# The order of the seven half products in a Strassen–Winograd second matmul: seventh product early, parts kept in the output blocks

## The chip, the cores and the metric

The kernel runs on one core of one Trainium2 chip. The metric is the device time of one execution in microseconds (us). An execution of it keeps five engines busy at once: PE (matmul), DVE (vector), ACT (activation), POOL (a second, slower vector engine) and SP, which here only issues DMAs. Each takes its own instructions strictly in the order in which the program lists them and waits on semaphores for the others.

## The reference

Eight batches of an attention between a block `x` (512 tokens, 8 heads of 64) and a state (32 rows) are computed in both directions, joined, and put through a two-layer MLP with SiLU:

```python
def _attn_ref(x, state):                       # x [8,8,512,64], state [8,8,32,64]
    scores = scale * np.matmul(x, state.transpose(0, 1, 3, 2))
    a = softmax(scores)
    xread = np.matmul(a, state)
    scores2 = scale * np.matmul(state, x.transpose(0, 1, 3, 2))
    a2 = softmax(scores2)
    sread = np.matmul(a2, x)
    return np.concatenate([xread, sread], axis=2)

def _moe_ref(x, w_in, w_out):                  # x [4352,512], w_in [512,2048], w_out [2048,512]
    h = x @ w_in
    g = h * (1.0 / (1.0 + np.exp(-h)))
    return g @ w_out
```

(The two softmaxes are written out in the original; they are shortened here.)

## The kernel before

**Units.** A batch's 512 rows of `xread` are one unit of work, b = 0 to 7; the rows of `sread` of all batches make a last, smaller unit 8. `w_in` is multiplied into the state beforehand: `W1[b]` = state times `w_in`, so the first matmul of the MLP is `aT[b]` (normalised attention weights, transposed) times `W1[b]`. It runs in 16 steps, "G1 steps" j = 0 to 15 (`upto`, `emit_G1`, L540): two matmuls of 512 columns into a PSUM tile `h1`, then one SiLU on ACT into `g` (L568). Tile `h1` has two buffers; a new step needs the buffer that is two steps old. The first eight SiLU results are the unit's `lo`, the other eight its `hi`.

**Second matmul.** For units 1 to 7 `g @ w_out` is done as seven half products (Winograd's form of Strassen's scheme), each 8 values of k with two matmuls of 256 columns (`Unit.mm`, L648): "a pair" below is these two matmuls. With A11, A21 the two halves of `lo` and A12, A22 those of `hi`, and S1 = A21 + A22, S2 = S1 − A11, S3 = A11 − A21, S4 = A12 − S2: P1 = A11·B11, P2 = A12·B21, P6 = S2·D2, P4 = A22·D4, P5 = S1·D1, P3 = S4·B22, P7 = S3·D3. The D's are differences of `w_out` (`t_weights`, tile `wt`), made once. S1 and S2 are tiles (`sums12`), S3 and S4 overwrite parts of `g` (`sums3`, `sums4`); all these sums run on DVE.

**PSUM.** P1, P6, P5 and P7 add up in one PSUM bank, `al`. P2, P4 and P3 each use the other bank, `be`, one after the other. After P1, P6 and P5 a copy of `al` is taken into an SBUF tile `snap` (`Unit.snap`); when a product in `be` is done, DVE adds it to a snap into a block of the unit's two output tiles `o_sb` (`block(i, c)`, 0 to 1 each). The last block, C22, is `al` after P7: `finish_last` copies it on ACT and adds on POOL, and this is done during the next unit's G1 steps (`j == lead + 1`). The banks have two tags, `o0` and `o1`; `al` takes the one with the unit's parity, so the roles swap from unit to unit.

**Order around a unit.** The program is scheduled by hand. In the G1 steps, `early` puts the pairs of P1 and then P2 between the steps. At the end come, in this order: the rest of P2; `group_a` (pieces of W1 for a later batch, `scores_t(m)`, and in some units `sread`) ahead of the last two pairs; P6; P4; P5; `group_b` (more pieces of W1); P3; P7. Six G1 steps of the next unit are put among the pairs of P3 and P7 (`LEADS = 6`). Unit 1 runs its `scores(2)` and `group_a` after P2 and P6, and units 1 and 7 have no `group_a` inside P2.

**Other work at fixed places of the G1 steps** (`j == lead + 1`, or right after unit 1's third step): on DVE `t_weights` (unit 1), `evict_state` (units 1 and 2), `norm_t(n)` (normalises the next unit's attention weights; one half runs on POOL), `spread_x`, `place_xm` (unit 7); on SP `fetch_x(m + 1)`, the load of a later `x`.

**SP's queue.** The loads of `x`, the stores of outputs (`out_half`) and all DMA transposes (`xT`, `aT`, `e`, `xs`) are issued by SP, one after the other; an entry whose semaphore has not come holds up all behind it. POOL casts the loaded `x` (`cast_x`, four instructions); SP then transposes it (`transpose_x`), and `scores_t` of that batch uses it.

Of the kernel before, what the change touches and what calls it, by code (L numbers as in the profile page):

```python
# [8 lines left out]
FP32 = mybir.dt.float32  # L9
# [9 lines left out]
B = 8  # L19
# [6 lines left out]
NFT = DF // 128  # L26
# [16 lines left out]
def kernel(  # L43
# [526 lines left out]
    def G2(b, tt, ft):  # L570
        if ft == 0:
            if b == 0 and tt >= 2:
                outs[tt] = psA.tile([128, DM], FP32, tag=f"a{tt - 2}", name="o_a")
            else:
                i = tt % 2
                outs[tt] = psO.tile([128, DM], FP32, tag=f"o{i}", name="o")
        nc.tensor.matmul(  # L577
            outs[tt][:],
            gt[b * NFT + ft][:, ds(128 * tt, 128)],
            w_out_sb[:, ft, :],  # L580
            start=(ft == 0),
            stop=(ft == NFT - 1),
            skip_group_check=True,
        )
# [23 lines left out]
    class Unit:  # L608
        def __init__(self, b):
            self.b = b  # L610
            self.lo, self.hi = gh[b, 0], None
            self.s1 = spool.tile([128, 8, 256], BF16, tag="s1", name="s1")
            self.s2 = spool.tile([128, 8, 256], BF16, tag="s2", name="s2")
            self.al = psO.tile([128, 2, 256], FP32, tag=f"o{b % 2}", name="o")
            self.be = None
            self.o = [
                opool.tile([128, 2, DM], FP32, tag=f"o_sb{i}", name="o_sb") for i in range(2)
            ]

        def snap(self, eng):  # L620
            t = spool.tile([128, 2, 256], FP32, tag=f"snap{len(self.kept) % 2}", name="snap")
            self.kept.append(t)
            copy(eng, t[:], self.al[:])

        kept = None

        def mm(self, p, k):
            hi, lo = self.hi, self.lo
            left, right = {
                1: (lambda: lo[:, k, 0:256], B11),  # L630
                2: (lambda: hi[:, k, 0:256], B21),
                3: (lambda: hi[:, k, 0:256], B22),
                4: (lambda: hi[:, k, 256:512], D4),
                5: (lambda: self.s1[:, k], D1),
                6: (lambda: self.s2[:, k], D2),
                7: (lambda: lo[:, k, 256:512], D3),
            }[p]
            left = left()
            if p in (2, 3, 4):
                if k == 0:  # L640
                    self.be = psO.tile(
                        [128, 2, 256], FP32, tag=f"o{1 - self.b % 2}", name="o"
                    )
                to, first = self.be, k == 0
            else:
                to, first = self.al, p == 1 and k == 0
            for t in range(2):
                nc.tensor.matmul(  # L648
                    to[:, t, :],
                    left[:, ds(128 * t, 128)],  # L650
                    right[:, k, :],
                    start=first and t == 0,
                    stop=(k == 7),
                    skip_group_check=True,
                )

        def sums12(self, k0, n):
            k = ds(k0, n)
            add(nc.vector, self.s1[:, k], self.lo[:, k, 256:512], self.hi[:, k, 256:512])
            sub(nc.vector, self.s2[:, k], self.s1[:, k], self.lo[:, k, 0:256])  # L660

        def sums4(self):
            for k0 in (0, 4):
                k = ds(k0, 4)
                sub(nc.vector, self.hi[:, k, 0:256], self.hi[:, k, 0:256], self.s2[:, k])

        def sums3(self):
            for k0 in (0, 4):
                k = ds(k0, 4)
                sub(nc.vector, self.lo[:, k, 256:512], self.lo[:, k, 0:256], self.lo[:, k, 256:512])  # L670

        def block(self, i, c):
            return self.o[i][:, :, ds(256 * c, 256)]
# [177 lines left out]

    PIECES_A = {1: 1, 2: 2, 3: 2, 4: 1, 5: 2, 6: 2}
    PIECES_B = {1: 3, 2: 3, 3: 3, 4: 3, 6: 2}
    LEADS = 6

    def finish_last(u):
        copy(nc.scalar, u.block(1, 1), u.al[:])
        add(nc.gpsimd, u.block(1, 0), u.block(1, 0), u.block(1, 1))
        u.out_half(1)

    def fetch_x(i):
        n = 4 if i < 6 else H
        for h in range(0, H, n):
            load_x(i, h, n, nc.sync)

    prev = None
    for b in range(1, B):
        n = b + 1
        m = n + 1
        u = Unit(b)  # L870
        u.kept = []
        lead = 3 if b == 1 else LEADS
        todo = [(1, k) for k in range(8)] + [(2, k) for k in range(8)]
        n_todo = len(todo)

        def early(j):
            while (
                todo
                and (8 * (todo[0][0] - 1) + todo[0][1]) <= j - 2
                and (n_todo - len(todo)) * (NFT - lead) < 13 * (j + 1 - lead)  # L880
            ):
                u.mm(*todo.pop(0))
                if len(todo) == 8:
                    u.snap(nc.vector)

        for j in range(lead, NFT):
            upto(NFT * b + j + 1)
            if j == 8:
                u.hi = gh[b, 1]
            if j == lead + 1:  # L890
                if prev is not None:
                    finish_last(prev)
                if b == 1:
                    transpose_x(3)
                    t_weights((2, 4, 3), 4, 4)
                    for v in range(2):
                        evict_state(v, nc.vector, 2, 2)
                    spread_x(2)
                elif n < B:
                    if b == 2:  # L900
                        for v in range(2):
                            evict_state(v, nc.vector, 4, 4)
                    norm_t(n)
                    spread_x(n)
                else:
                    for half in range(2):
                        place_xm(half, nc.vector)
                if 1 < b and m + 1 < B:
                    fetch_x(m + 1)
            early(j)  # L910
            if j == 13:
                u.sums12(0, 4)
        srs = SREAD_AT.get(b, ())

        def group_a():
# [3 lines left out]
            ps_sr = sread(srs, bank if m < B else new_h) if srs else None  # L919
            return pss, ps_sr  # L920

        u.sums12(4, 2)
        while todo:
            if len(todo) == 2 and 1 < b < B - 1:
                made = group_a()
            u.mm(*todo.pop(0))
        u.sums12(6, 2)
        add(nc.vector, u.block(0, 0), u.be[:], u.kept[0][:])
        if b == 1:
            for hg in range(2):  # L930
                scores(2, hg)
# [7 lines left out]
        if 1 < b and m + 1 < B:  # L939
            for c in range(4):  # L940
                cast_x(m + 1, nc.gpsimd, c, 1)
        def sread_g1(step):
            if n == B:
                upto(NFT * B + (step + 1) * NFT // 34)

        step = 0
        for k in range(8):
            u.mm(6, k)
            if n == B and k > 5:
                sread_g1(step)  # L950
                step += 1
        u.snap(nc.scalar)
        if b == 1:
            for hg in range(2):
                norm(2, hg)
# [1 line left out]
            made = group_a()  # L957
            exps_t(m)
            fetch_x(m + 1)
        if b > 1:  # L960
            u.sums4()
        if n < B:
            if m < B:
                nc.scalar.activation(warm[:], busy[:, 0:1], func=SILU, bias=0.0)
            w1_out(*made[0][0])
            if srs:
                sread_out(srs, made[1])
            for piece in made[0][1:]:
                w1_out(*piece)
        if b == 1:  # L970
            u.sums4()
        for k in range(8):
            u.mm(4, k)
            sread_g1(step)
            step += 1
        add(nc.vector, u.block(1, 0), u.be[:], u.kept[1][:])
        if 1 < b and m + 1 < B:
            transpose_x(m + 1)
        u.sums3()
        for k in range(8):  # L980
            u.mm(5, k)
            sread_g1(step)
            step += 1
        u.snap(nc.scalar)
        sub(nc.gpsimd, u.block(1, 0), u.block(1, 0), u.kept[2][:])
        if b in PIECES_B:
            c = PIECES_B[b]
            pss = w1_next(2) + (w1_next(1, new_h) if c == 3 else [])
            for i in (2, 0, 1)[3 - c :]:
                w1_out(*pss[i])  # L990
        for p in (3, 7):
            for k in range(8):
                u.mm(p, k)
                sread_g1(step)
                step += 1
                i = 8 * (p == 7) + k
                if n < B and i % 2 == 1 and 0 < i // 2 <= LEADS:
                    upto(NFT * n + i // 2)
            if b == 1 and p == 3:
                for c in range(4):  # L1000
                    cast_x(m + 1, nc.gpsimd, c, 1)
                transpose_x(m + 1)
            if p == 3:
                add(nc.vector, u.block(0, 1), u.be[:], u.kept[2][:])
                u.out_half(0)
        prev = u
        for ft in range(NFT):
            gt.pop(NFT * b + ft)
    finish_last(prev)
    for ft in range(NFT):  # L1010
        upto(NFT * B + ft + 2)
        G2(B, 0, ft)
# [32 lines left out]
```

## Time and profile before

| what | value |
|---|---|
| median of 3 runs | 203.37 us (203.17 to 203.37) |
| the profiled execution, its own time | 203.08 us |
| its span in the profile | 201.3 us |
| DVE busy | 126.9 us (63%) |
| ACT busy | 141.0 us (70%) |
| POOL busy | 60.8 us (30%) |
| G1 matmuls, L540, 252 of 512 columns | 73.8 us busy |
| half products, L648, 784 of 256 columns | 111.7 us busy |
| granted TensorE clock | 1.00 |

Busy times of matmuls overlap, since they are pipelined; the distance from the start of one to the start of the next tells their real price. Between two 512-column matmuls in a row it is 0.216 us, between two of 256 columns 0.109 us. So a G1 step costs PE 0.433 us, a pair 0.218 us, and a half product of eight pairs 1.75 us. The span leaves 1.8 us outside, which is the same work's start and end around the core's instructions.

### The profile page before, as it was taken

The numbers are of one execution on the slowest core, as the hardware profiler recorded it, in microseconds if no ns is written. First come the engines' busy times: TensorE is split into PE (matmuls) and PEld (weight loads), VectorE is DVE, ScalarE is ACT, GpSimd is POOL, SyncE is SP. The second block draws the span as 40 slices with busy tenths as digits, with TensorE's granted clock in tenths as the row PEclk, the third lists the DMA queues.
The fourth block names the chain that finished last, engine by engine and source line by source line (L and its number), as shares of the span: only waits on it lengthen the run. The fifth ranks groups of instructions, "written<-read, shape, count | busy, mean of one in ns | idle before, by whom it ended". The sixth has DMA issues, their size and how long they took to land.

```text
span 201.3 us, 4661 instructions
## 1 busy us (share of the span) xinstructions
PE 195.3 (97%) x1912; PEld 129.6 (64%) x1912; DVE 126.9 (63%) x244; ACT 141.0 (70%) x251; POOL 60.8 (30%) x79
## 2 busy tenths in 40 slices
PE   7799999999999999999999999999999999999992
PEld 2444445456866586668666776668666766688862
DVE  3862756999988797558864798187617972832101
ACT  2875667899787897789868777897784478545420
POOL 8674343730425504240804071400140022002020
PEclk9999999999999999999999999999999999999999
DMA  5999999994282797759164947142214020200222
GB/s 185 193 202 206 242 266 346 247 239 96 35 220 80 234 261 138 208 160 242 45 182 135 253 50 215 45 118 55 104 44 116 7 87 27 104 3 0 104 111 101
DMA packets 40965, 28.71 MB, mean 143 GB/s; under 512 B 27376, under 2 KB 37616, under 8 KB 40944
## 3 DMA queue, kind: packets, MB, share of 16 engines
q1 hardware_dynamic: 34736, 20.65, 38.4%
q0 software_dynamic: 5920, 7.64, 18.4%
q8 instruction: 15, 0.25, 0.5%
q10 hardware_dynamic: 288, 0.13, 0.3%
q14 instruction: 6, 0.05, 0.1%
HBM read 17.43 MB, written 8.91 MB: 131 GB/s over the span
## 4 chain that ended last, share of the span: by engine, by line
PE 94%; DMA 2%; DVE 1%; ACT 1%; issue 0%
PE o L648 43%; PE h L540 27%; PE o L577 5%; PE ps_w L473 5%; PE h L558 3%; PE o_a L577 3%; DMA x_f<-in_x_dram 2%; PE o_part L698 2%; PE ps_xt L257 1%; PE ps_sr L420 1%; PE ps_sc L310 1%; ACT xT L160 1%; PE ps_busy L168 1%; PE ps_scT L336 1%; PE ps_at L402 1%; PE h L522 0%
## 5 line engine op out<-in xcount | busy, mean ns | idle before, releaser
L568 ACT ACTIVATE g<-h 128x512 bf16<-128x512 f32 (+1 forms) x142 | 80.1, 575 | 29.0 <-PE h L540 20.1
L648 PEld LDWEIGHTS <-g 128*128 128x128 bf16 x560 | 53.7, 98 | 33.2 <-issue 3.1
L540 PE MATMUL h<-aT,W 128*128 128x512 bf16 x252 | 73.8, 379 | 0.1
L648 PE MATMUL o<-w_out_sb,g 128*128 128x256 bf16 x336 | 53.5, 273 | 0.1
L648 PE MATMUL o<-wt,g 128*128 128x256 bf16 x224 | 30.8, 273 | 0.0
L540 PEld LDWEIGHTS <-W 128*128 128x128 bf16 x252 | 24.4, 98 | 7.6 <-issue 0.7
L162 POOL CAST x_nat<-x_f 128x512 bf16<-128x512 f32 x24 | 17.4, 764 | 34.0 <-DMA x_f<-in_x_dram 28.3
L648 PE MATMUL o<-wt,s 128*128 128x256 bf16 x224 | 27.4, 273 | 0.0
L594 DVE TENSOR_TENSOR o_sb<-o,snap 128x512 f32<-128x512 f32 x21 | 14.5, 689 | 18.7 <-PE o L648 15.5
L162 DVE CAST W<-ps_w 128x512 bf16<-128x512 f32 (+1 forms) x35 | 21.8, 665 | 6.4 <-PE ps_w L473 6.4
L648 PEld LDWEIGHTS <-s 128*128 128x128 bf16 x224 | 21.9, 98 | 2.5
L591 POOL TENSOR_TENSOR o_sb<-o_sb,snap 128x512 f32<-128x512 f32 x7 | 8.9, 1269 | 37.3 <-ACT snap L160 37.3
L594 POOL TENSOR_TENSOR o_sb<-o_sb 128x512 f32<-128x512 f32 x7 | 8.9, 1266 | 36.7 <-ACT o_sb L160 36.7
L162 DVE COPY snap<-o 128x512 f32<-128x512 f32 x7 | 4.8, 691 | 23.3 <-PE o L648 19.1
L160 ACT ACTIVATE W<-ps_w 128x512 bf16<-128x512 f32 (+1 forms) x31 | 16.2, 580 | 2.8 <-PE ps_w L473 2.8
L160 ACT ACTIVATE snap<-o 128x512 f32<-128x512 f32 x14 | 8.4, 597 | 14.0 <-PE o L648 9.7
L577 PE MATMUL o<-w_out_sb,g 128*128 128x512 bf16 x48 | 13.2, 380 | 0.0
L577 PEld LDWEIGHTS <-g 128*128 128x128 bf16 x80 | 7.3, 98 | 8.7 <-issue 0.8
L594 DVE TENSOR_TENSOR s<-g 128x512 bf16<-128x512 bf16 (+1 forms) x21 | 11.5, 549 | 1.7 <-ACT g L568 1.6
L591 DVE TENSOR_TENSOR s<-s,g 128x512 bf16<-128x512 bf16 (+1 forms) x21 | 10.8, 514 | 0.7
L473 PE MATMUL ps_w<-w_in_sb,stT 64*32 64x512 bf16 (+1 forms) x264 | 10.2, 375 | 0.0
L591 DVE TENSOR_TENSOR g<-g 128x1024 bf16<-128x1024 bf16 x14 | 10.1, 759 | 0.0
(93 smaller groups left out, 191.6 us busy)
## 6 DMA issues: line engine op xcount, KB each, us to landing
out_dram<-o_sb SPq DMA_DIRECT2D x14, 512.0 KB, 2.8
x_f<-in_x_dram SPq DMA_DIRECT2D x6, 512.0 KB, 5.3
x_f<-in_x_dram POOLq DMA_DIRECT2D x2, 1024.0 KB, 11.6
x_f<-in_x_dram SPq DMA_DIRECT2D x2, 1024.0 KB, 6.5
w_out_sb<-in_moe_w_out_dram POOLq DMA_DIRECT2D x6, 256.0 KB, 11.3
w_in_sb<-in_moe_w_in_dram POOLq DMA_DIRECT2D x3, 512.0 KB, 10.6
out_dram<-o_sb SPq DMA_DIRECT2D x5, 256.0 KB, 5.7
x_f<-in_x_dram POOLq DMA_DIRECT2D x2, 512.0 KB, 14.6
```

The costliest lines, as they stand in the source:

```text
L160: nc.scalar.activation(dst, src, func=COPY, bias=0.0)
L162: eng.tensor_copy(dst, src)
L168: nc.tensor.matmul(ps[:], busy[:, 0:128], busy[:], start=True, stop=True, skip_group_check=True)
L473: nc.tensor.matmul(pss[f, hg][ds(32 * s, 32), 0:n], stT[ds(r, 64), b, h // 2, s % 2, :], w_in_sb[ds(r, 64), h // 2, ds(f, n)], start=True, ...
L540: nc.tensor.matmul(h_ps[k][:], W1[b][:, hg, ds(128 * ft, 128)], aT[b][:, hg, :, :], start=(hg == 0), stop=(hg == 1), skip_group_check=True,)
L558: nc.tensor.matmul(ps[:, 0:256], w_in_sb[:, kt, ds(128 * ft, 128)], xmT[:, :, kt].rearrange("p t n b -> p t (n b)"), start=(kt == 0), stop ...
L568: nc.scalar.activation(gt[k], ps[:, 0:n], func=SILU, bias=0.0)
L577: nc.tensor.matmul(outs[tt][:], gt[b * NFT + ft][:, ds(128 * tt, 128)], w_out_sb[:, ft, :], start=(ft == 0), stop=(ft == NFT - 1), skip_gr ...
L591: eng.tensor_tensor(dst, a, c, op=SUB)
L594: eng.tensor_tensor(dst, a, c, op=ADD)
L648: nc.tensor.matmul(to[:, t, :], left[:, ds(128 * t, 128)], right[:, k, :], start=first and t == 0, stop=(k == 7), skip_group_check=True,)
L698: nc.tensor.matmul(ps[:, 0:n], gt[b * NFT + ft][:, ds(128 * tt, 128)], w_out_sb[:, ft, cols], start=(ft == 0), stop=(ft == NFT - 1), skip_ ...
```

## The change

- P7 moves from the last place to the second: after P1, between the G1 steps, since it needs `lo` alone. It gets the bank `be`, which P2, P4 and P3 then use after it. `al` is always `o1` and `be` always `o0`.
- The difference for P7 (`sums3`) moves to the G1 steps: its first half at step 5, its second at step 9, on DVE. S2 is made directly from A22 − S3 in one instruction (`sums2`); S1 = S2 + A11 follows later (`sums1`, after P6's instructions).
- The snaps are gone: P1, P7, P6 and P5 are copied into the output blocks (`keep`), and later adds work in place. POOL adds P7 to U2 = P1 + P6 (`block(1, 0)`) and the copy of `al` after P5 to the P7 block. Stores go out in the same unit: half 1 after P5, half 0 after P3.
- Order at a unit's end: rest of P7; DVE copies P7; S2; `group_a` whole (units 2 to 6) with its evictions; all of P2; P6; P4; `group_b` (units 2 to 6; in unit 1 after P5); P5; P3. Five G1 steps of the next unit go in: one after P5, four among P3's pairs (unit 1: two after the second pair of P3).
- `fetch_x(m + 1)` moves from step 7 to step 5, ahead of `norm_t`'s transpose in SP's queue. The other work of step 7 moves to step 9; in unit 2 half of `evict_state` goes to POOL. In unit 1, D3 is made at step 5 and D2 and D4 at step 9, behind `evict_state` and `spread_x`.
- Unit 8's G1 steps in unit 7 are spread over 26 pairs instead of 34.

```diff
@@ Unit
-            self.al = psO.tile([128, 2, 256], FP32, tag=f"o{b % 2}", name="o")
+            self.al = psO.tile([128, 2, 256], FP32, tag="o1", name="o")
-        def snap(self, eng):
-            t = spool.tile([128, 2, 256], FP32, tag=f"snap{len(self.kept) % 2}", name="snap")
-            self.kept.append(t)
-            copy(eng, t[:], self.al[:])
+        def keep(self, eng, i, c):
+            copy(eng, self.block(i, c), self.al[:])
-            if p in (2, 3, 4):
+            if p in (7, 2, 4, 3):
                 if k == 0:
+                    self.be = psO.tile([128, 2, 256], FP32, tag="o0", name="o")
-        def sums12(self, k0, n):
-            add(nc.vector, self.s1[:, k], self.lo[:, k, 256:512], self.hi[:, k, 256:512])
-            sub(nc.vector, self.s2[:, k], self.s1[:, k], self.lo[:, k, 0:256])
+        def sums3(self, k0, n):
+            sub(nc.vector, self.lo[:, k, 256:512], self.lo[:, k, 0:256], self.lo[:, k, 256:512])
+        def sums2(self, k0, n):
+            sub(nc.vector, self.s2[:, k], self.hi[:, k, 256:512], self.lo[:, k, 256:512])
+        def sums1(self):
+            for k0 in (0, 4):
+                add(nc.vector, self.s1[:, k], self.s2[:, k], self.lo[:, k, 0:256])
@@ the G1 steps
-    LEADS = 6
+    LEADS = 5
-        todo = [(1, k) for k in range(8)] + [(2, k) for k in range(8)]
+        todo = [(p, k) for p in (1, 7) for k in range(8)]
-                and (n_todo - len(todo)) * (NFT - lead) < 13 * (j + 1 - lead)
+                and (n_todo - len(todo)) * (NFT - lead) < 16 * (j + 1 - lead)
                 u.mm(*todo.pop(0))
                 if len(todo) == 8:
-                    u.snap(nc.vector)
+                    u.keep(nc.vector, 0, 0)
-            if j == lead + 1:
-                if prev is not None:
-                    finish_last(prev)
+            if j == max(lead, 5):
                 if b == 1:
+                    t_weights((3,), 4, 4)
                     transpose_x(3)
-                    t_weights((2, 4, 3), 4, 4)
+                u.sums3(0, 4)
+                if 1 < b and m + 1 < B:
+                    fetch_x(m + 1)
+            if j == 9:
+                u.sums3(4, 4)
+                if b == 1:
                     for v in range(2):
                         evict_state(v, nc.vector, 2, 2)
                     spread_x(2)
+                    t_weights((2, 4), 4, 4)
                 elif n < B:
                     if b == 2:
                         for v in range(2):
-                            evict_state(v, nc.vector, 4, 4)
+                            evict_state(v, (nc.vector, nc.gpsimd)[v], 4, 4)
                     norm_t(n)
                     spread_x(n)
-                if 1 < b and m + 1 < B:
-                    fetch_x(m + 1)
             early(j)
             if j == 13:
-                u.sums12(0, 4)
+                u.sums2(0, 4)
@@ the end of the unit
-        u.sums12(4, 2)
         while todo:
-            if len(todo) == 2 and 1 < b < B - 1:
-                made = group_a()
             u.mm(*todo.pop(0))
-        u.sums12(6, 2)
-        add(nc.vector, u.block(0, 0), u.be[:], u.kept[0][:])
+        copy(nc.vector, u.block(1, 1), u.be[:])
+        u.sums2(4, 2)
+        if 1 < b < B - 1:
+            made = group_a()
+        u.sums2(6, 2)
+        if 1 < b < B - 1:
+            out_a()
+        for k in range(8):
+            u.mm(2, k)
+        add(nc.vector, u.block(0, 0), u.block(0, 0), u.be[:])
...
+        units(6)
+        u.keep(nc.scalar, 1, 0)
+        add(nc.gpsimd, u.block(1, 0), u.block(1, 0), u.block(1, 1))
         if b == 1:
             for hg in range(2):
                 norm(2, hg)
                 transpose_a(2, hg)
             made = group_a()
             exps_t(m)
             fetch_x(m + 1)
+            out_a()
+        u.sums1()
+        units(4)
+        add(nc.vector, u.block(1, 0), u.block(1, 0), u.be[:])
         if 1 < b and m + 1 < B:
             transpose_x(m + 1)
+        u.sums4()
+        if b > 1:
+            group_b()
+        units(5, {7: 1} if b > 1 else {})
+        u.keep(nc.scalar, 0, 1)
+        add(nc.gpsimd, u.block(1, 1), u.block(1, 1), u.block(0, 1))
+        u.out_half(1)
+        if b == 1:
+            group_b()
+        units(3, {1: 2, 3: 3, 5: 4, 7: 5})
+        if b == 1:
+            for c in range(4):
+                cast_x(m + 1, nc.gpsimd, c, 1)
+            transpose_x(m + 1)
+        add(nc.vector, u.block(0, 1), u.block(0, 1), u.be[:])
+        u.out_half(0)
```

`group_b` is now a small function with the same body; `out_a` holds the evictions of `group_a`; `units(p, leads)` issues the eight pairs of product p and, after the pairs named in `leads`, G1 steps of the next unit up to that number. The number of matmuls on PE does not change (3826 PE instructions, weight loads among them, in both).

## The prediction

> **What bounds the kernel now.** I read the page's busy times and chain first, then the order of time on each engine around the ends of units 1, 2 and 7.
>
> ```profile
> PE 195.3 (97%) x1912; PEld 129.6 (64%) x1912; DVE 126.9 (63%) x244; ACT 141.0 (70%) x251; POOL 60.8 (30%) x79
> PE 94%; DMA 2%; DVE 1%; ACT 1%; issue 0%
> ```
>
> PE sets the time: 94% of the chain that ended last. The change keeps every matmul, so it wins only what PE waits for today, and loses what it will wait for. PE's order of time at the end of unit 2:
>
> ```profile
> 68.19 0.38 PE L648 MATMUL o<-w_out_sb,g 128*128 128x256 bf16 x2
> 68.41 0.59 PE L540 MATMUL h<-aT,W 128*128 128x512 bf16 x2
> 68.84 0.60 PE L648 MATMUL o<-w_out_sb,g 128*128 128x256 bf16 x4
> 69.37 0.63 PE L473 MATMUL ps_w<-w_in_sb,stT 64*32 64x512 bf16 x16
> 69.81 0.40 PE L336 MATMUL ps_scT<-xT,stT 64*32 64x512 bf16 x8
> 70.15 0.61 PE L648 MATMUL o<-w_out_sb,g 128*128 128x256 bf16 x4
> ```
>
> Starts follow each other without a hole: G1 step 0.433, pair 0.218, `group_a` 0.87 (69.28 to 70.15, the entry of 0.09 included). Distances of starts beyond the usual 0.109 give what PE loses: 0.20 in unit 1 (at 47.06), 0.20 in unit 7 (174.35), where P2's last pair waits for the last SiLU with no `group_a` to cover it, and 0.09 in each of units 2 to 7 (64.75 the first), just behind `finish_last`'s ACT copy: 0.94 in all. **That is the whole prize** if every new wait is hidden.
>
> **The change, part by part.** Latencies from the trace: last matmul's start to a DVE instruction that waits for it 0.38 (58.24 to 58.62), to an ACT one 0.30 (49.71 to 50.01); engine to PE 0.05; G1 step's start to its SiLU's end 1.23 (173.38 to 174.61).
>
> (a) Removed: the 0.94. P2's end needs no fresh SiLU, and `finish_last` is gone from the G1 steps.
>
> (b) P7's copy now stands ahead of P2, in bank `o0`. PE could start P2 right after P7 in unit 7. From step 15: P7's last pair at 0.433, its second matmul at 0.54; DVE at 0.92; the copy 0.69 (as `snap` today), so P2 at 1.66, where PE was free at 0.65: 1.0 lost. With `group_a` (0.87) between, PE is free at 1.52: units 3 and 5 lose 0.14 each. Unit 4 has one piece of W1 only: its second `scores_t` tile waits for the last SiLU (1.28 after step 15 instead of 0.96), 0.3 lost. Unit 6 has `sread` as cover, none. Sum 1.6; bounds 1.2 (0.2 less in units 3 and 5 and in latencies) and 1.8.
>
> (c) Unit 1: the copy of P7 is behind a full DVE queue. Today:
>
> ```profile
> 39.62 1.93 DVE L591 TENSOR_TENSOR wt<-w_out_sb,wt 128x1024 bf16<-128x1024 bf16 x2
> 41.46 1.09 DVE L591 TENSOR_TENSOR wt<-w_out_sb 128x1024 bf16<-128x1024 bf16 x1
> 42.48 1.81 DVE L162 COPY stT<-st_x 64x64 bf16<-64x64 bf16 x8
> 44.32 0.69 DVE L162 COPY x_rows<-x_nat 128x2048 bf16<-128x2048 bf16 x1
> 44.93 0.68 DVE L162 COPY snap<-o 128x512 f32<-128x512 f32 x1
> 45.53 0.68 DVE L594 TENSOR_TENSOR s<-g 128x1024 bf16<-128x1024 bf16 x1
> ```
>
> DVE has no hole here. By these starts: D3 1.02, state copies 1.84, `x_rows` 0.61, D2 with D4 1.84, P1's copy 0.60, a half sum 0.71; half of `sums3` 0.64 (two take 1.28 in a row at 75.06). New order: D3 39.62 to 40.64, `sums3` first half to 41.3, then a hole: its second half needs SiLU 7, whose step starts at 41.11 (40.89 today, one pair more before it), so 42.4 to 43.05; state copies 44.9, `x_rows` 45.5, D2 and D4 47.35, P1's copy 47.95, `sums2` 48.65, P7's copy 49.35. PE finishes P7 at 47.40: step 15 is at 46.09 with 12 pairs before it and will have 15 (46.75), plus 0.433 and 0.218. P2 waits from 47.4 to 49.4: **2.0**. If D2 and D4 take 1.5 (the weights' group has a mean of 0.816, and POOL is silent then) 1.65. I take 2.0, the row itself.
>
> (d) `aT` for unit 2. Count from S, the end of P2 in unit 1, where `scores(2)` starts (S = 47.60 today). Today, POOL and then SP:
>
> ```profile
> 50.40 2.05 POOL L386 TENSOR_TENSOR an<-exp_nat,rc 128x512 bf16<-128x512 bf16 x2 [8.39 <-DVE rc L384]
> 62.70 3.20 POOL L162 CAST x_nat<-x_f 128x512 bf16<-128x512 f32 x4 [5.67 <-DMA xs<-xm]
> ```
>
> SP's own instructions in the same stretch (start, duration, what it issues):
>
> ```profile
> 51.48 3.73 SPq L396 DMA_TRANSPOSE aT<-an  x2
> 55.30 1.26 SPq L352 DMA_TRANSPOSE e<-eT  x1
> 56.65 1.11 SPq L112 DMA_DIRECT2D x_f<-in_x_dram  x2
> 57.86 3.67 SPq L448 DMA_TRANSPOSE xs<-xm  x3
> 65.93 1.65 SPq L147 DMA_TRANSPOSE xT<-x_nat  x1
> 67.68 1.01 SPq L676 DMA_DIRECT2D out_dram<-o_sb  x2
> ```
>
> The new POOL add of `block(1, 0)` stands ahead of both `an` in POOL's queue and waits for ACT's copy after P6: P6's last matmul S+2.11, copy S+2.41 to 3.01, add to 4.35 (1.27 as the POOL add at 55.73), first `an` to 5.4 (it ends at S+3.8 today), second to 6.4. SP: first transpose issued S+5.4 to 7.85 (2.42 today), second to 9.15, landed S+10.3 (2.35 after its issue, as today). PE reaches step 0 at S+9.05: `scores` 0.47, P6 1.75, `group_a` 1.53 (49.82 to 51.35), P4 1.75, P5 1.75, `group_b` 0.87, two pairs 0.44, and 0.48 before P5, since `sums1` is queued behind `sread_out`'s DVE work (S+5.25) and gives its first half at S+5.95. Step 0's second matmul, due S+9.26, waits till S+10.35. Together 0.48 + 1.08 = **1.55**. If the first transpose issues in 1.22 as the second does, all lands at S+9.1 and 0.48 is left. I take the same row's 2.42.
>
> (e) Unit 2: the longest new chain. P1's copy now writes the output tile, so it waits until unit 1's half 0 has been stored; behind it on DVE wait `sums2` and P7's copy, and P2 behind that. In SP's order the store stands behind the transpose `xT` of batch 4, which waits for POOL's cast, which waits for the load. Load: S+10.6 and 11.2 (SP after `aT` and `e`), landed 5.25 after the second issue (57.24 to 62.49 today): S+16.45. Cast from 16.65: 2.28 at best (four of 0.61, at 78.48), 3.20 above; I take 2.75, since DVE's `sums3` and `norm_t` run beside it as at 62.70. Transpose S+19.45 to 21.1, store issued 21.2, landed 3.2 later (67.68 to 70.79; 82.48 to 85.74) at 24.4. Then P1's copy 0.60, `sums2` 0.71, P7's copy 0.69, latencies 0.1: P2 at S+26.5. PE would be ready: step 0 ends S+10.55, step 1 10.98, three times (two pairs and a step) 0.87 gives step 5 at S+13.6; eleven steps and sixteen pairs 8.26; `group_a` 0.87: S+22.7. **3.75 lost**; bounds 3.15 (short issue, cast 2.28) and 4.2 (cast 3.20). The same wait hides that `xT` and half of `evict_state`, on POOL now (no row for such a copy there; DVE's are 0.27 each, POOL's casts of four times the length 0.61 to 1.07: 1 to 4 us for four), come late for `scores_t`: they would be done by S+23.8 at worst, and after the cover is gone would cost up to 0.6.
>
> The Trainium skill, "SBUF — State Buffer", section "Who interferes with whom", says that DVE and POOL share a port pair as an exclusive lock: DVE with two SBUF inputs blocks a POOL instruction that reads SBUF. The rows side with it only in part: a cast beside DVE's two-input work takes 1.07 instead of 0.61, not 0.61 plus the whole 0.76 of such a sum. By the rule the cast beside the moved `sums3` would take 0.3 more and the time with it; by the rows the 2.75 stands.
>
> (f) Later in unit 2: `cast_x(5)` is ahead of POOL's add. Its load is issued S+21.7 and 22.5, landed 28.4, cast to 30.9, add to 32.2, DVE's add in place 32.9, S4's halves 33.55 and 34.2, first W1 eviction 34.85. PE needs S4 for P3 after P5 and step 0 at S+34.8, and the evicted bank for step 1 at 35.2: nothing lost, 0.7 at the slow bounds. In units 3 and 4 the load goes out at step 6 and lands two us before the cast is due; S4 is ready 1.2 us ahead of P3, W1's bank 0.5 ahead of step 1. ACT in those units gives its copy after P6 in time for POOL. Nothing is charged there; the cover is P4, `group_b` and P5 (4.4 us).
>
> (g) In unit 7 the tail after P3 (16 matmuls of 0.216 and the `o_part` columns, 7 us) covers the last add and store; nothing.
>
> Sum: −0.94 + 1.6 + 2.0 + 1.55 + 3.75 = +8.0. The profiled execution took 203.08 (span 201.3, 1.8 around it), 0.3 under the median 203.37: 211.0 by the first, 211.3 by the second; I say **211.0**. Low ends: −0.94 + 1.2 + 1.65 + 0.48 + 3.15 = +5.5, 208.6; high: −0.94 + 1.8 + 2.0 + 1.55 + 4.2 + 0.7 = +9.3, 212.7.
>
> **Rivals.** First: the store of unit 1's half 0 is not late, so (e) falls to the plain 0.14 of (b). It takes a load landed and cast 3.6 us sooner. For it: DMA issues vary by two (1.22 and 2.42 for equal transposes), and the first `x` load before it took 4.1. Against: four waits in a row, each in program order. Then +4.4 or, with short issues, +3.0: 206.4 to 207.5. Chance 0.17.
>
> Second, faster: DVE is never the late one. The place is P2's start in units 1 to 7; the price is the 0.94 that (a) frees. It decides if P7's copy ends before PE is through `group_a` everywhere, that is, if the wait from P7 to P2 is 0.13 or less on average over seven units. For it: DVE is only 63% busy. Against: in unit 7 nothing stands between, and 0.38 + 0.69 cannot vanish; in unit 1 DVE has no hole. 202.4, chance 0.10, and 0.03 that gain and loss cancel.
>
> Third: (f) turns into a wait, the slow cast holding POOL's add, DVE's adds and S4 in unit 2 and again in 3, at 1 us or more each: above 213.1, chance 0.09.
>
> **Numbers.** Forecast 0.61 for 208.6 to 213.1, its own range. For 8 in 10 the range goes down over part of the first rival: 206.0 to 213.3. Faster by over 0.2% (the spread that runs of this kernel can tell from nothing) 0.10, within it 0.03, slower 0.87.
>
> **What would show it.** In the profile after: PE's largest waits before L642 at the start of P2 in unit 1 (2 us), unit 2 (3 to 4 us) and unit 7 (1 us), each ended by DVE's `o_sb<-o` copy; step 0 of unit 2 waiting for `aT`; DVE idle ahead of unit 2's first `o_sb` copy with a DMA as its releaser. Units 3 to 6 about as long as now. I am wrong if unit 2's copy of P1 finds its store landed, or if P2 in unit 1 starts before 48.

## The result, and the profile after

The changed kernel takes 211.16 us (median of 4 runs, 210.53 to 212.70) against 203.37 us before (203.17 to 203.81): a ratio of 1.039, 95% interval 1.033 to 1.045. The profiled execution took 212.70 us with a span of 210.8 us, 9.5 us more than the span before. Times of the experiments below are medians of all executions; their ratios leave out the slowest execution of e1, e5, e7 and e10, each over 1.5% longer than the fastest of its kernel, with a mean clock of 0.984 to 0.992.

The page's busy times, chain, and two rows of its 40 slices (5.3 us each; digits are tenths):

```profile
PE 197.8 (94%) x1893; PEld 131.3 (62%) x1912; DVE 133.3 (63%) x240; ACT 137.9 (65%) x244; POOL 64.1 (30%) x83
PE   7899999997899949999999999999999999899993
PEclk9999999999999966999999999999999999999999
PE 77%; DMA 11%; DVE 6%; POOL 2%; issue 1%; ACT 1%; POOLq 0%; DVEq 0%
```

PE's share of the chain fell from 94% to 77%; DMA, DVE and POOL stand in it now. PE is 40% busy in one slice, the 15th (73.8 to 79.0 us), and the granted clock is down in that slice and the next. Who PE waited for between 40 and 190 us (waiting instruction, releaser, us in total, times, longest):

```profile
PE o L642 <- DVE o_sb L162: 4.8, 3, 2.9
PE o L642 <- DVE s L594: 0.7, 2, 0.4
PE h L540 <- ACT W L160: 0.2, 1, 0.2
```

The three waits for DVE's copy of P7 are those of units 1, 2 and 7, as forecast. Unit 2 on PE, in order of time (start, duration, line, operation, count; in brackets the idle time before and what ended it):

```profile
72.38 0.38 PE L642 MATMUL o<-wt,g 128*128 128x256 bf16 x2
72.69 0.63 PE L473 MATMUL ps_w<-w_in_sb,stT 64*32 64x512 bf16 x16
73.13 0.50 PE L336 MATMUL ps_scT<-xT,stT 64*32 64x512 bf16 x8
76.52 3.57 PE L642 MATMUL o<-w_out_sb,g 128*128 128x256 bf16 x16 [2.89 <-DVE o_sb L162]
79.89 2.34 PE L642 MATMUL o<-wt,s 128*128 128x256 bf16 x10
```

DVE at the same time, in the same columns:

```profile
71.64 0.69 DVE L366 TENSOR_TENSOR an<-e,rcn 128x512 bf16<-128x512 bf16 x1
72.25 1.54 DVE L162 COPY x_rows<-x_nat 128x2048 bf16<-128x2048 bf16 x1
74.58 0.69 DVE L162 COPY o_sb<-o 128x512 f32<-128x512 f32 x1 [0.79 <-DMA out_dram<-o_sb]
75.19 0.68 DVE L591 TENSOR_TENSOR s<-g 128x1024 bf16<-128x1024 bf16 x1
75.79 0.69 DVE L162 COPY o_sb<-o 128x512 f32<-128x512 f32 x1
```

SP's DMA queue a little earlier (start, time that the issue holds the queue, line, operation):

```profile
68.95 1.69 SPq L147 DMA_TRANSPOSE xT<-x_nat  x1
70.74 0.54 SPq L673 DMA_DIRECT2D out_dram<-o_sb  x1
```

P1's copy (74.58) waits for the store that SP issued at 70.74 and that landed at 74.49; S2's first half and P7's copy (75.79) follow, and P2 starts at 76.52. Its 16 matmuls take 3.57 us instead of 1.91: each costs 0.213, twice the 0.109 of the page before. A table by stage (stretch, its length, then busy us of PE, weight loads, DVE, ACT and POOL, granted clock, DMA share, GB/s) shows why:

```profile
66.00:73.40 7.40, 7.35 (x68) 4.45 (x66) 6.11 (x9) 6.03 (x11) 5.89 (x9) 1.00 0.71 215
73.40:76.50 3.10, 0.23 (x8) 0.10 (x1) 2.31 (x5) 3.07 (x6) 0.00 (x0) 0.86 0.91 231
76.50:82.40 5.90, 5.88 (x28) 4.21 (x28) 4.00 (x7) 0.27 (x1) 2.28 (x4) 0.50 0.74 147
82.40:88.00 5.60, 5.55 (x66) 4.17 (x65) 2.88 (x5) 3.76 (x7) 1.27 (x1) 1.00 0.42 96
```

After the 3 us without a matmul, the clock is at 0.50 until 82.4: 27 matmuls (15 of P2, 12 of P6) lose 0.104 each, 2.8 us. The prediction's sum has no term for that.

The two other places. Unit 1, DVE ahead of P2:

```profile
45.72 1.41 DVE L591 TENSOR_TENSOR wt<-w_out_sb,wt 128x1024 bf16<-128x1024 bf16 x2
47.05 0.68 DVE L162 COPY o_sb<-o 128x512 f32<-128x512 f32 x1
47.65 0.68 DVE L591 TENSOR_TENSOR s<-g 128x1024 bf16<-128x1024 bf16 x1
48.25 0.68 DVE L162 COPY o_sb<-o 128x512 f32<-128x512 f32 x1
```

And PE in unit 1, with its waits in brackets:

```profile
47.51 0.38 PE L642 MATMUL o<-wt,g 128*128 128x256 bf16 x2
48.98 1.91 PE L642 MATMUL o<-w_out_sb,g 128*128 128x256 bf16 x16 [1.09 <-DVE o_sb L162]
56.70 1.05 PE L642 MATMUL o<-wt,s 128*128 128x256 bf16 x8 [0.30 <-DVE s L594]
58.16 1.05 PE L642 MATMUL o<-wt,s 128*128 128x256 bf16 x8 [0.41 <-DVE s L594]
```

Here P7's copy is the last of DVE's full queue, and P5 (56.70, 58.16) waits for both halves of S1. By distances of starts, the losses of PE are: P2 of unit 1 1.25, P5's halves 0.47 and 0.57, the first steps of unit 2 together 0.54, P2 of unit 2 2.96 and the half clock 2.8, unit 4's `scores_t` 0.31, P2 of unit 7 0.94, and 0.09 at `scores_t` in units 2, 3 and 5. The 0.94 that PE lost before, in eight places, is gone. Sum: +9.2; the other 0.3 is in the first 40 us, where nothing was changed (PE is 0.5 us later at 36 us, after the first loads).

### The profile page after: what moved, and what is told of

It is laid out like the page before. It is cut to its first block, busy times and chain, and to the rows that moved or that the text cites. A ratio compares the mean times of both kernels' runs of the same rounds, so it can differ in the third digit from the quotient of the medians.

```text
span 210.8 us, 4631 instructions
## 1 busy us (share of the span) xinstructions
PE 197.8 (94%) x1893; PEld 131.3 (62%) x1912; DVE 133.3 (63%) x240; ACT 137.9 (65%) x244; POOL 64.1 (30%) x83
## 4 chain that ended last, share of the span: by engine, by line
PE 77%; DMA 11%; DVE 6%; POOL 2%; issue 1%; ACT 1%; POOLq 0%; DVEq 0%
PE o L642 41%; PE h L540 20%; DMA x_f<-in_x_dram 9%; PE h L558 3%; PE ps_w L473 3%; PE o L577 3%; DMA out_dram<-o_sb 2%; PE o_part L695 2%; PE o_a L577 1%; DVE o_sb L162 1%; PE ps_sr L420 1%; PE ps_xt L257 1%; DVE stT L162 1%; DVE s L594 1%; POOL w_in_sb L153 1%
## 5 line engine op out<-in xcount | busy, mean ns | idle before, releaser
L540 PE MATMUL h<-aT,W 128*128 128x512 bf16 x237 | 69.5, 379 | 0.3 <-ACT W L160 0.2
L642 PE MATMUL o<-w_out_sb,g 128*128 128x256 bf16 x336 | 50.3, 280 | 5.1 <-DVE o_sb L162 4.8
L594 POOL TENSOR_TENSOR o_sb<-o_sb 128x512 f32<-128x512 f32 x14 | 17.7, 1266 | 78.6 <-ACT o_sb L160 78.6
L594 DVE TENSOR_TENSOR o_sb<-o_sb,o 128x512 f32<-128x512 f32 x21 | 14.4, 685 | 38.1 <-PE o L642 29.0
L642 PE MATMUL o<-wt,g 128*128 128x256 bf16 x224 | 33.3, 273 | 0.4
L642 PE MATMUL o<-wt,s 128*128 128x256 bf16 x224 | 28.9, 281 | 0.7 <-DVE s L594 0.7
L160 ACT ACTIVATE o_sb<-o 128x512 f32<-128x512 f32 x16 | 9.5, 595 | 20.3 <-issue 12.7
L366 POOL TENSOR_TENSOR an<-e,rcn 128x512 bf16<-128x512 bf16 x5 | 7.7, 1540 | 24.4 <-DVE rcn L364 23.4
L162 DVE COPY o_sb<-o 128x512 f32<-128x512 f32 x15 | 10.3, 684 | 1.7 <-DMA out_dram<-o_sb 0.8
L594 DVE TENSOR_TENSOR s<-s,g 128x1024 bf16<-128x1024 bf16 x14 | 10.1, 764 | 0.0
```

The costliest lines, as they stand in the source:

```text
L160: nc.scalar.activation(dst, src, func=COPY, bias=0.0)
L162: eng.tensor_copy(dst, src)
L366: eng.tensor_tensor(a[:, hg], e2[b][:, hg], rc[:, hg].to_broadcast([128, 4, 4, NS]), op=MULT)
L540: nc.tensor.matmul(h_ps[k][:], W1[b][:, hg, ds(128 * ft, 128)], aT[b][:, hg, :, :], start=(hg == 0), stop=(hg == 1), skip_group_check=True,)
L594: eng.tensor_tensor(dst, a, c, op=ADD)
L642: nc.tensor.matmul(to[:, t, :], left[:, ds(128 * t, 128)], right[:, k, :], start=first and t == 0, stop=(k == 7), skip_group_check=True,)
```

## The experiments

All are edits of the changed kernel. Their ratios are against the kernel before, run beside them (203.14 to 203.32 us in median).

**e1: the store first.** In unit 1 the store of half 0 goes ahead of the cast and transpose of x(4).

```diff
+        add(nc.vector, u.block(0, 1), u.block(0, 1), u.be[:])
+        u.out_half(0)
         if b == 1:
             for c in range(4):
                 cast_x(m + 1, nc.gpsimd, c, 1)
             transpose_x(m + 1)
-        add(nc.vector, u.block(0, 1), u.block(0, 1), u.be[:])
-        u.out_half(0)
```

> Unit 1's store of half 0 goes ahead of the transpose of x(4) in SP's queue; nothing else moves. Theory A (the store's landing alone holds P2 of unit 2): P2's wait there falls from 2.9 us to 0.2 or less and the half clock behind it is gone: some 5 us less than the changed kernel. Theory B (DVE's own queue is nearly as late, free at 73.79 us against the store's landing at 74.49): the wait falls by 0.8 only, to 2.1 us; the clock may still drop. I hold B: time 0.8 us lower if the clock drops all the same, up to 3.6 lower if it does not.

208.75 us, ratio 1.025 (1.020 to 1.030). DVE in unit 2, in its profile:

```profile
72.16 1.54 DVE L162 COPY x_rows<-x_nat 128x2048 bf16<-128x2048 bf16 x1
73.62 0.68 DVE L162 COPY o_sb<-o 128x512 f32<-128x512 f32 x1
```

P2 of unit 2 on PE:

```profile
75.55 1.91 PE L642 MATMUL o<-w_out_sb,g 128*128 128x256 bf16 x16 [2.08 <-DVE o_sb L162]
```

P1's copy no longer waits for a DMA, it starts as soon as DVE is free. The wait fell by 0.8 (2.96 to 2.15 by starts) and not to nothing: theory B. The clock stayed at 1.00 through unit 2 in this profile, and the time fell by 2.4 us in median. (One of the four executions, without a profile, had a mean clock of 0.992 and took 212.62.)

**e2: x_rows late.** In unit 2 `spread_x` goes behind the evictions after P7's copy.

```diff
                     norm_t(n)
-                    spread_x(n)
+                    if b > 2:
+                        spread_x(n)
...
             out_a()
+        if b == 2:
+            spread_x(n)
```

> Unit 2's copy into x_rows (1.54 us on DVE, ahead of P1's copy) is put behind the evictions after P7's copy; the store stays late. Theory A (store): no change, P2's wait stays 2.9 us and the time within 0.3 us of the changed kernel. Theory B in its strong form (DVE's queue alone): the wait falls by 1.5 us. With the two in a row as a maximum: no change. I hold no change.

211.41 us, ratio 1.039 (1.033 to 1.045): no change. P1's copy on DVE:

```profile
74.56 0.69 DVE L162 COPY o_sb<-o 128x512 f32<-128x512 f32 x1 [2.40 <-DMA out_dram<-o_sb]
```

DVE now idles 2.40 us before this copy, which starts when the store has landed; PE waits 3.50 in this execution.

**e3: both edits, of e1 and of e2.**

> Both: the store first and the copy into x_rows late. If the wait is the later of two chains, it now falls to 0.7 to 1.0 us (P7's copy is then bound by P7's end, 0.38 + 0.69 after it, less group_a), more than the two single steps together (0.8 and 0). Clock stays at 1.00: 4.5 to 5 us less than a profile of the changed kernel with the clock drop, 2.2 less than one without. If a third chain is behind them (x(4)'s transpose for scores_t, the state copies on POOL), the wait stays over 1.5 us and PE waits at scores_t.

208.94 us, ratio 1.026 (1.022 to 1.030). P2's wait is 0.90, and P1's copy starts at 72.10. So the wait in unit 2 is the later of two chains, the store's and DVE's own queue: taking away one wins 0.8 or nothing, both 2.1. But the time is no better than e1's, since part of it comes back 8 us later, on DVE:

```profile
81.23 0.69 DVE L594 TENSOR_TENSOR o_sb<-o_sb,o 128x512 f32<-128x512 f32 x1 [2.29 <-POOL o_sb L594]
81.83 1.28 DVE L591 TENSOR_TENSOR g<-g,s 128x1024 bf16<-128x1024 bf16 x2
83.04 1.88 DVE L162 CAST W<-ps_w 128x512 bf16<-128x512 f32 x3
```

POOL's add of P7 stands behind the casts of x(5), DVE's add waits 2.29 us for it, the eviction of W1 comes at 83.04, and step 1 of unit 3 loses 0.75 for its bank. That is (f) of the prediction, hidden there by the longer wait before it.

**e4: the gap filled.** Twelve matmuls on zeros between `group_a` and P2 of unit 2; their result is not used.

```diff
+        if b == 2:
+            turn[0] += 1
+            ps = bank([128, 512], FP32, "ps_busy")
+            for _ in range(12):
+                nc.tensor.matmul(ps[:], busy[:, 0:128], busy[:], start=True, stop=True, ...)
```

> Twelve idle matmuls of 512 columns (2.6 us) are put between group_a and P2 of unit 2, where PE waits 2.9 us; their result is not used. Theory C (the granted clock halves because PE idles there): the clock is 1.00 throughout in every run, P2 starts at the same time as in the changed kernel (within 0.2 us), and the time falls by what the half clock cost: 2.8 us against the profile with the clock at 0.984, 0.5 to 1.6 against runs at 0.997 to 0.991. Theory D (the clock is lowered for another reason, load or chance): the clock drops as often as before and the time is the same.

210.63 us, ratio 1.035 (1.031 to 1.038); the profiled execution 209.99 against 212.70. By stage:

```profile
66.00:73.20 7.20, 7.20 (x68) 4.42 (x66) 6.07 (x9) 5.83 (x11) 5.89 (x9) 1.00 0.73 218
73.20:76.50 3.30, 3.02 (x20) 1.26 (x13) 2.35 (x5) 3.27 (x6) 0.00 (x0) 1.00 0.94 249
76.50:82.40 5.90, 5.83 (x72) 4.84 (x71) 4.63 (x8) 2.17 (x4) 3.86 (x5) 1.00 0.67 135
```

P2 on PE:

```profile
76.57 1.91 PE L642 MATMUL o<-w_out_sb,g 128*128 128x256 bf16 x16
```

It starts where it did (76.52), and the clock stays at 1.00: 72 matmuls between 76.5 and 82.4 where there were 28. All four executions show a mean clock of 1.000, those of the changed kernel 0.984, 0.991, 0.992 and 0.997. Four executions alone could be chance; counted over all kernels it is not. Where the profile has PE waiting 2.5 us or more before P2 of unit 2 (the changed kernel, e2, e5, e6, e7, e10), 17 of 25 executions have a mean clock of 0.992 or less; where PE waits 0.9 or less there or is kept busy (e3, e4, e8, e9, e11), none of 44 is under 0.996, nor is any of the 58 of the kernel before that ran beside the experiments. (e9's profile, at 0.998, has the half clock only after the last matmul, so 0.996 to 0.998 need not be a drop in unit 2.) The gap, not chance, lowers the clock: theory C.

**e5: a bank of its own.** P2 of units 1 and 7 accumulates in a third bank and does not wait for P7's copy.

```diff
+                    if p == 2 and self.b in (1, B - 1):
+                        self.be = bank([128, 2, 256], FP32, "o")
+                    else:
+                        self.be = psO.tile([128, 2, 256], FP32, tag="o0", name="o")
```

> P2 of units 1 and 7 gets a PSUM bank of its own, so it does not wait for P7's copy; nothing else moves. The step that P7's copy stands on the path with 0.38 + 0.69 us: unit 1's wait of 1.25 and unit 7's of 0.94 us vanish, 2.2 us off the changed kernel. Rival (the wait only moves on: P6 then waits for S2, which DVE makes after that copy): P6 of unit 1 and 7 waits up to 1 us each and less than 1 us is won. I expect 2.0 to 2.2 with a wait of 0.2 or less at P6.

208.76 us, ratio 1.024 (1.019 to 1.030): 2.4 less in median. The two executions with a mean clock of 1.000 took 208.15 and 208.40, those of the changed kernel (e10) 209.67 and 210.86: 1.3 to 2.7 less, with the forecast of 2.0 to 2.2 inside. Both waits are gone, none stands at P6; unit 2's is still there (3.1).

**e6: S1 first.** In unit 1 `sums1` goes ahead of the evictions of `group_a` on DVE.

```diff
             fetch_x(m + 1)
-            out_a()
-        u.sums1()
+            u.sums1()
+            out_a()
+        else:
+            u.sums1()
```

> In unit 1 the two S1 sums go ahead of the W1 eviction and sread's evictions on DVE, so P5's two waits there (0.47 and 0.57 us) fall to 0.2 or less. Theory A (waits add up, as in my sum): about 0.9 us less than the changed kernel. Theory B (unit 2's P2 waits for a chain of POOL, SP and DMA that PE's lateness does not move): P2 of unit 2 waits the same 0.9 us longer, and the time is the same, or longer by what a longer half clock costs. I hold B.

211.44 us, ratio 1.038 (1.033 to 1.043): nothing won. PE's waits from 56 to 78 us:

```profile
PE o L642 <- DVE o_sb L162: 3.5, 1, 3.5
PE ps_scT L336 <- DMA xT<-x_nat: 0.7, 1, 0.7
PE h L540 <- DMA aT<-an: 0.4, 1, 0.4
```

P5's two waits are gone and PE comes earlier, so step 0 waits for `aT`, `scores_t` for `xT` and P2 longer for the copy. Waits ahead of a chain that does not go through PE are no terms of a sum: theory B. (Unit 1's wait at P2, which e5 removes, stands before the start of that chain, and it does count.)

**e7: an first.** In unit 1 POOL does both `an` before its add.

```diff
-        add(nc.gpsimd, u.block(1, 0), u.block(1, 0), u.block(1, 1))
         if b == 1:
             for hg in range(2):
                 norm(2, hg)
                 transpose_a(2, hg)
+        add(nc.gpsimd, u.block(1, 0), u.block(1, 0), u.block(1, 1))
```

> In unit 1 POOL does both an before the add into block(1,0), as before the change. The load of x(4), its cast, its transpose and the store come 1.2 us earlier. If the store's chain starts where I put it, P2's wait in unit 2 falls by 0.8 us (then DVE's queue, free at 73.8, is the later one) and S1's sums are less disturbed by POOL; the time falls by 0.8 to 1.3 us. If the chain starts elsewhere (the load's own duration, SP's xs transposes), the wait of 2.9 us stays.

209.53 us, ratio 1.027 (1.021 to 1.033): 1.6 less in median, more than the 0.8 to 1.3 of the forecast, among executions that differ in clock too (1.000 in two, 0.992 in two). P2 of unit 2 on PE:

```profile
75.21 3.15 PE L642 MATMUL o<-w_out_sb,g 128*128 128x256 bf16 x14 [2.49 <-DVE o_sb L162]
```

P2 starts 1.3 us earlier than in the changed kernel, but its wait is 2.55 by starts, 0.4 less and not the 0.8 forecast, since PE comes earlier too: P5's second wait has gone. Without the matmuls at half clock the losses add up to 6.5 us against 7.3. P1's copy still waits for the store, which has landed 1.3 us earlier: POOL's add does stand in that chain.

**e8, e9, e11: the repairs together.** e8 has e1, e2, e5, e6, e7, the first of unit 2's state copies at step 5, and POOL's casts behind its add. What is new in it:

```diff
@@ unit 2, step 5
                 u.sums3(0, 4)
+                if b == 2:
+                    evict_state(0, nc.vector, 4, 4)
...
                     if b == 2:
-                        for v in range(2):
-                            evict_state(v, (nc.vector, nc.gpsimd)[v], 4, 4)
+                        evict_state(1, nc.gpsimd, 4, 4)
...
-        if 1 < b and m + 1 < B:
-            for c in range(4):
-                cast_x(m + 1, nc.gpsimd, c, 1)
...
         add(nc.gpsimd, u.block(1, 0), u.block(1, 0), u.block(1, 1))
+        if 1 < b and m + 1 < B:
+            for c in range(4):
+                cast_x(m + 1, nc.gpsimd, c, 1)
```

> All of it: unit 1's store first, x_rows late and the state copies early in unit 2, own bank for P2 in units 1 and 7, S1 first and an first in unit 1, and POOL's casts after its add into block(1,0) in all units. Every wait that I found in units 1, 2 and 7 should be 0.2 us or less, the clock 1.00. Sum: the kernel before less the 0.94 us that the change frees, plus 0.5 us for P7's copy in units 2 to 5 and up to 0.5 left over in units 1 and 2: 202.9 to 203.6 us, within 0.3% of the kernel before. Rival: a wait that I have not seen stands behind these, and it stays over 205.

205.29 us, ratio 1.011 (1.007 to 1.014): a miss by 1.7, on the side of its rival. The losses left: 1.33 at step 1 of unit 2, where DVE's eviction of W1 is late (S1's and S4's sums take 2.47 and 2.36 us for two instead of 1.28, beside POOL's `an` and add), and 0.27 in each of units 2 to 4 by the same (S4 beside the casts). e9 gives that eviction to ACT in unit 1 and moves the casts in unit 2 only:

```diff
+                    if b == 1:
+                        engs = (nc.scalar, nc.scalar) if i == 2 else (nc.vector, nc.vector)
```

> The version with all repairs, with its two leftovers mended: in unit 1 the W1 piece in the SiLU banks is evicted by ACT alone (DVE's eviction came 1.33 us late there, behind sums that POOL slowed) and the other two by DVE alone; POOL's casts go behind its add in unit 2 only (behind it in units 3 and 4 they slowed DVE's S4 and cost 0.27 each). Expected: 1.3 + 0.5 us less than that version's 205.29, that is 203.4 to 203.8; not below the kernel before by more than 0.2%, since P7's copy still costs 0.1 to 0.3 in units 2 to 5. Rival: something outside these waits holds 205 (the waits over 0.04 us sum to 2.5 there against 1.1 in the kernel before, so 0.4 of its 1.8 us of span is not in them); then 204.5 or more.

203.42 us, ratio 1.001 (1.000 to 1.003). PE waits for one thing between 40 and 190 us:

```profile
PE o L645 <- DVE g L591: 0.2, 1, 0.2
```

e11 goes for the last two known losses: `sread` goes ahead of `scores_t`, and ACT takes that eviction in unit 2 too.

```diff
             pss = w1_next(PIECES_A[b])
+            ps_sr = sread(srs, bank if m < B else new_h) if srs else None
             if m < B:
                 scores_t(m)
-            ps_sr = sread(srs, bank if m < B else new_h) if srs else None
...
-                    if b == 1:
+                    if b in (1, 2):
                         engs = (nc.scalar, nc.scalar) if i == 2 else (nc.vector, nc.vector)
```

> The mended version with its two last known waits taken out: in units 1 and 4 sread goes ahead of scores_t in group_a (scores_t waits 0.31 us for the last SiLU in unit 4), and in unit 2, too, the W1 piece in the SiLU banks is evicted by ACT alone (0.27). 0.5 us less than the mended version: 202.9, within 0.3% of the kernel before; if its waits are no longer the measure, the same 203.4.

202.92 us, ratio 0.999 (0.997 to 1.000): as expected, and not told apart from the kernel before.

**e10: the changed kernel again**, with no edit.

> The changed kernel again, unaltered, to see how often and how long its clock is halved: theory C (a PE gap of 3 us decides it, by where the gap falls): every run has a halved stretch of about 3.4 or 6.8 us or none, and the time goes with it: 209.9 without, 211.3 with the shorter, 212.7 with the longer. Theory D (chance unrelated to the gap): some runs of the kernel before would show the same.

211.67 us, ratio 1.038 (1.033 to 1.043). Its profile has one stretch of 6.83 us at half clock in unit 2, after a wait of 3.43, and 212.48 us; two executions had a mean clock of 1.000 and took 209.67 and 210.86. So the gap does not lower the clock every time, and the second of these is 1 us over what theory C gave; that is left open. Theory D's sign did not come: the 17 executions of the kernel before that ran beside this one have mean clocks of 0.996 to 1.000.

## Why the prediction was right, and where it was right by luck

It said 211.0 and slower, by P2's waits in units 1, 2 and 7 and unit 2's first steps; 211.16 was measured, and these are the places. The single terms are less good:

| step | forecast, us | measured in the profile, us |
|---|---|---|
| (a) PE's old waits gone | −0.94 | −0.94 |
| (b) P7's copy ahead of P2, units 3 to 7 | 1.6 | 1.4 (0.94 in unit 7, 0.31 in unit 4; 0.09 each in units 3 and 5, at `scores_t` and not at P2) |
| (c) unit 1, DVE's queue | 2.0 | 1.25 |
| (d) to step 0 of unit 2 | 1.55 | 1.58, for another reason |
| (e) P2 of unit 2 | 3.75 | 3.05 (2.96, and 0.09 at `scores_t`) |
| half clock after (e) | not seen | 2.8 |

(c) was mis-sized: D2 and D4 took 1.33 from start to start (45.72 to 47.05), not the 1.84 of the row that I took; the other price in the text, 1.5, was nearer, since POOL was silent. PE also came to P2 0.3 later than counted. Of the 1.25, 0.94 is the mere latency and length of the copy, as unit 7 shows.

(d) named a wrong cause for over two thirds of it. The first `aT` transpose was issued in 1.2 us, not 2.42, so `aT` landed at 59.90, before step 0 at 60.72. The 0.48 before P5 was right (0.47). The remaining 1.11 has two other causes. One is 0.57 at P5's second half: POOL's `an`, now pushed back, ran beside S1's sums, and both were stretched. POOL in the changed kernel:

```profile
53.82 1.28 POOL L594 TENSOR_TENSOR o_sb<-o_sb 128x512 f32<-128x512 f32 x1 [12.17 <-ACT o_sb L160]
55.05 2.50 POOL L386 TENSOR_TENSOR an<-exp_nat,rc 128x512 bf16<-128x512 bf16 x2
```

DVE beside it:

```profile
55.94 2.16 DVE L594 TENSOR_TENSOR s<-s,g 128x1024 bf16<-128x1024 bf16 x2
```

`an` takes 2.50 for two instead of 2.05, S1 2.16 instead of 1.3, and P5's second half waits another 0.57; in e7, with `an` ahead, S1 takes 1.43 and this wait is gone. The other is the 0.54 of unit 2's first steps:

```profile
60.72 0.81 PE L540 MATMUL h<-aT,W 128*128 128x512 bf16 x3 [0.20 <-ACT W L160]
```

Step 0 waits for ACT's eviction of a piece of W1 from `group_b`; it now comes two pairs behind `group_b`, where it came four pairs behind, and step 2 waits for the SiLU of step 0, which is late for the same reason. This 0.54 stands in e7 as well, so it is not POOL's doing. e6 shows that the forecast wait for `aT` would have come had PE been earlier.

(e) had the right chain: load, cast (2.78; 2.75 was taken), transpose, store, P1's copy, S2, P7's copy. It was 0.7 long, mostly by the transpose's issue of 2.42 in (d) that it was built on. What the text did not see is that DVE's queue in unit 2 is nearly as late as the store (free at 73.79, store landed at 74.49), which e1 to e3 show: the mechanism has two legs, and the forecast named one. The cover given for (f) held only because of this wait; e3 takes it away and (f) costs 0.75.

The three sizes over by 0.2, 0.75 and 0.7, 1.65 together, are paid back by the clock, which was missing: 2.8 in the profile, which is the slowest of the four executions, and by estimate 1.7 in one with a single stretch of 3.41 us (16 matmuls of 0.104), as e2's profile has it at the mean clock, 0.992, of two of the others (0.991 and 0.992). So the places and the waits for P7's copy were forecast, and that 211.0 was so close was luck. Without a clock drop the changed kernel would be near 210, as e4 (210.63, profile 209.99) shows.

Rivals: the first (store not late, 206.4 to 207.5) is what e1 tries, and 208.75 says that DVE would have been next. The second (faster) fails at unit 7 alone. The third, (f), did not come here. The range given ends at 213.1, where the sum of the high ends gives 212.7; the working has no term for the difference.

The Trainium skill, "SBUF — State Buffer", "Who interferes with whom", was weighed for POOL's casts, and there the row's figure held: 2.78 for the four. The prediction took that row to speak in part against the rule. It does not: in the kernel before, the cast began at 63.25, 0.10 after DVE's sum (63.15 to 63.86), and ended at 64.33, 0.47 after that sum's end, so it had only the rest of the sum to wait for, not the whole. For DVE, too, the rule of an exclusive lock was the better guide: `x_rows` took 1.54 instead of 0.68, and it ended at 73.79, 0.55 after POOL's `an` beside it (71.74 to 73.24), as if it had stood still until then.

## What to carry to other kernels

An output block that doubles as scratch takes over the block's store as a wait, and that store has everything ahead of it on its DMA queue: follow the queue before saving the copy. Where a buffer is handed from one product to the next, put work of another bank between the last matmul and the next user for the copy's latency and length (0.94 us here), and check which units have none. Before adding up waits, ask whether they stand in front of one chain that does not go through the bound engine; if so, only the last of them counts, and mending the earlier ones moves the time into it.

## What the hardware showed that was not expected

A wait of 2.5 to 3.5 us between matmuls can halve the granted clock: stretches of 3.41 us (e2, e5, e7) and 6.83 us (the changed kernel, e6, e10) at 0.50 in the profiles; in e1, with a gap of 2.15, none. The Trainium skill, "TensorE: Matmul & The Clock Gate", "What's actually happening", has a gate that watches activity in windows of about 3.4 us and halves the clock after an idle one. The stretches are one and two such windows long, which agrees; but no whole idle window was needed, since the wait in e7 was only 2.55 us.

The clock records of the traces say more. From the first record at full clock to the drop it is 71.68 us in the changed kernel, e2 and e6, 68.27 in e7 and e10, 64.85 in e5: 21, 20 and 19 times 3.41 us, as if counted in fixed windows. In the window ahead of the drop PE was idle for 1.99 us (e10), 2.00 (the changed kernel), 2.28 (e7), 2.56 (e5), 2.69 (e2) and 3.00 (e6); without a drop the most was 1.96, in e1. Where the next window held 0.90 to 1.39 us more of the gap, the half clock lasted 6.83 us; where it held 0.21 or nothing, 3.41. So the same gap may cost two windows, one or none, by where it falls. This is read off nine profiles; no run moves the gap within the windows, and 1.96 against 1.99, with the ends of matmuls modelled, names no sharp limit.

DVE and POOL slow each other in both directions beside work on SBUF: S1 or S4 in pairs 2.0 to 2.5 us instead of 1.3, `x_rows` 1.54 instead of 0.68, `an` on POOL 1.5 instead of 1.05. The single rows look like waiting, not like running slower: S1's second half ended at 58.10, 0.55 after POOL's `an` (57.55), and in e8 three halves of S4 ended 0.54 or 0.55 after the POOL instruction that had begun before them (58.96 after 58.41, 79.20 after 78.66, 80.22 after 79.68). Of the misses here, 0.57 us in (d) and the one of e8 are this.
